# Attention and SwiGLU on one core: seven PSUM banks as one tensor, and a shifted array made on GpSimd

## The chip, the cores and the metric

The kernel runs on one core of one Trainium2 chip. The metric is the device time of one execution in microseconds; three runs of the kernel before are known. A profile of one more execution shows the engines: PE (TensorE), PEld (its weight loads), DVE (VectorE), ACT (ScalarE), POOL (GpSimd) and SP (SyncE, which issues most DMAs).

## The reference

For x of 2048 rows and 512 columns (bf16), 32 heads of 16 columns:

```python
qkv = x @ wqkv                                    # q, k, v for 32 heads
scores = einsum("bhqd,bhkd->bhqk", q, k) * 16 ** -0.5
a = (softmax(scores) @ v, heads put together) @ wo
b = (silu(x @ w_gate) * (x @ w_up)) @ w_down      # 1792 wide
g = sigmoid((x * gate_w).sum(-1))
return g * a + (1 - g) * b
```

The head size of 16 makes the exponentials of 32 x 2048 x 2048 scores the bulk of the work.

## The kernel before, in words

The attention is cut into 32 *units*: four blocks of 512 queries by eight groups of four heads. A unit has 16 *key tiles* of 128 keys, so there are 512 key tiles. The scores of a key tile are four banks of PSUM, one for each head, with the 128 keys on the partitions and 512 queries along the bank.

Each key tile goes one of two ways.

- **ScalarE's way.** `choose()` and `emit_group()` make a *score group*: two matmuls (`score()`) into two neighbouring banks `s_t`, then one exponential of 128 x 1024 into `e_all`, of which 22 banks' worth are kept. Two such double tiles are used in turn (`WIDTHS = (2, 2)`).
- **VectorE's way.** `emit_d()` makes the scores of one head into a single bank `d_t`. Such a matmul can *ride* with a score group: it uses other rows of the array than the two heads of the group. VectorE reads the bank once (`first()` in `emit_d`: a multiplication and an addition, written as 16-bit integers, so that the bits are an approximate exponential in bf16) into a quarter of an array y of 2048 columns. When the four banks of a key tile are in, VectorE refines the approximation. A *four-array* tile (`groups[n] == 4`) gets three copies of y, shifted by integer additions of 25, 56 and 94 (`copy()`), and the four arrays together stand for the exponential. A *two-array* tile (`groups[n] == 2`) gets two bit masks (`bits()`) and one product (`product()`). `quad()` decides: a four-array tile is taken when TensorE has had `SPARE` us to spare. The arrays lie in seven homes (`take_home()`, `home()`, `drop()`); the seventh is part of `wd_t` or `kaug`, so that the profile names these too.

The *PV steps* (`pv()`) multiply with the values, four matmuls in four column tiles into `o_ps`: one step for a key tile of ScalarE, two or four for one of VectorE. When all steps of a unit are done it is closed (`close()`, `post()`), normalised and projected. The FFN's matmuls, the projections for q, k and v, and the output are chains of *pieces* that a `Pacer` gives out by deadlines.

All the order is settled when the kernel is built. A planner in Python keeps a clock for each engine (`plan.pe`, `plan.dve`, `plan.act`), adds a price for each instruction, and emits the one that fits next; `ordered()` ties each instruction to the one before it on its engine, so the engines run just this order, each waiting where its data is late. Prices: 0.217 us for a slot on TensorE, `FLIP` 0.105 us each time that its tiling changes between score groups (rows) and the others (columns), 0.6 us for a bank read or a copy on VectorE, 1.135 us for a product, 0.064 + 0.4265 us per bank for an exponential. `fill_dve()` chooses VectorE's next work: bank reads (`d_wait`, paid by `pay_d()`), copies and the like (`vops`, `pay_v()`), or evictions for the other chains (`owed`, `later()`, `pay()`). `v_unit()` and `wants()` say whether VectorE can take another key tile: it does as long as its own clock lets it finish in time, so the split between ScalarE and VectorE follows from the prices.

PSUM has eight banks. One holds `o_ps`. Four are the two double tiles `s_t`, three (`NM = 3`, `m_tile()`, `m_free()`) are single banks for `d_t` and all chains. Each is a tile of its own pool, and the framework derives the waits from the tiles. GpSimd only fills constants at the start.

In the profile nearly all instructions have the line of a helper (L168 `mm`, L171 `act`, L180 VectorE and the queue), so groups are told apart by tile names.

Of the kernel before, what the change touches and what calls it, by code (L numbers as in the profile page):

```python
# [13 lines left out]
U16 = mybir.dt.uint16  # L14
F16 = mybir.dt.float16
# [64 lines left out]
def kernel(  # L80
# [35 lines left out]
    EB = 10  # L116
    NE = 22
    WIDTHS = (2, 2)
    NM = 3
# [11 lines left out]
    MUL_US = 1.135  # L131
    LATEST = 0.64
# [3 lines left out]
    SPARE = 0.3  # L136
# [12 lines left out]
    ps_s = ctx.enter_context(tc.tile_pool(name="ps_s", bufs=1, space=bass.MemoryType.PSUM))  # L149
    ps_m = [ctx.enter_context(tc.tile_pool(name=f"ps_m{i}", bufs=1, space=bass.MemoryType.PSUM)) for i in range(NM)]  # L150
    ps_o = ctx.enter_context(tc.tile_pool(name="ps_o", bufs=1, space=bass.MemoryType.PSUM))


    last_of = {}

    def ordered(ins):
        i = ins.ins
        if i.engine in last_of:
            tc.add_manual_dep(
                i, last_of[i.engine].name,  # L160
                mybir.DependencyInfo(mybir.DependencyClass.NoSync, mybir.DependencyReason.DATA),
                reason="order",
            )
        last_of[i.engine] = i
        return ins

    def mm(*args, **kw):
        return ordered(nc.tensor.matmul(*args, **kw))  # L168

    def act(*args, **kw):  # L170
        ordered(nc.scalar.activation(*args, **kw))  # L171

    class Ordered:
# [4 lines left out]
        def __getattr__(self, name):  # L178
            f = getattr(self.engine, name)
            return lambda *a, **kw: ordered(f(*a, **kw))  # L180

    vec = Ordered(nc.vector)
    queue = Ordered(nc.sync)
# [99 lines left out]

    kb = const.tile([P, NB], F32, name="kb")
# [8 lines left out]
    class Plan:  # L293
        pe = dve = act = 0.0
# [8 lines left out]
    banks = [0.0] * NM  # L303
    held = [None] * NM
    s_free = [0.0] * len(WIDTHS)
    turns = [0]

    def s_tile(i, name):
        return ps_s.tile([P, WIDTHS[i] * QBW], F32, tag=f"s{i}", name=name)
# [12 lines left out]
    def later(cost, f, ready=None, key=None):  # L322
# [5 lines left out]
        owed.insert(sum(o[0] <= ready for o in owed), (ready, cost, f, c, key))  # L328

    def spend_v(cost, ready=0.0, key=None):  # L330

        if key is not None and key == plan.last:
            cost += 0.13
        plan.last = key
        plan.dve = max(plan.dve, ready) + cost

    def pay(i=0):
        ready, cost, f, c, key = owed.pop(i)
        spend_v(cost, ready, key)
        keep, plan.chain = plan.chain, None  # L340
        f()
        plan.chain = keep
# [18 lines left out]
    def m_tile(name):  # L361
        while m_ready() is None:
            stuck()
        i = min((i for i in range(NM) if banks[i] is not None), key=lambda i: banks[i])
        plan.pe = max(plan.pe, banks[i])
        banks[i] = None
        held[i] = ps_m[i].tile([P, QBW], F32, tag=f"m{i}", name=name)
        return held[i]

    def m_free(ps, t):  # L370
        i = [h is ps for h in held].index(True)
        banks[i], held[i] = t + DVE_PE, None

# [10 lines left out]
    def force(c):  # L384
        for a in c.after + c.begun:
# [146 lines left out]
    def q_pieces(qb, b):  # L532
# [11 lines left out]
        def end(p, me):  # L544
# [7 lines left out]
            def mag():  # L552
# [3 lines left out]
                later(0.21, weigh, plan.dve, ("q", b))  # L556
# [5 lines left out]
            later(0.21, mag, plan.dve, ("q", b))  # L562
# [3 lines left out]
    def q0_pieces(qb):  # L566
# [3 lines left out]
        def landed(p):  # L570
            st["p"] = p
            later(0.6, mag, key=("aq", qb))
            later(0.21, clear, key=("aq", qb))
# [20 lines left out]
    def variants(p, to, q, more=()):  # L594
# [10 lines left out]
        later(0.4, select, key=key)  # L605
# [3 lines left out]
    def gate_end():  # L609
# [8 lines left out]
        later(0.5, end, plan.act + ACT_DVE)  # L618
# [113 lines left out]
    def choose():  # L732

        i = turns[0] % len(WIDTHS)
        if s_free[i] is None:
            flush_act()
        late = max(plan.pe, horizon() - LATEST, s_free[i])
        w = WIDTHS[i]
        if au == UNITS - 1:
            w = min(w, 4 * (hi[au] - at_) - quarter)  # L740
        want = wants()
        open_ = sorted(b for b in banks if b is not None and b <= late)
        n = max(0, min(want, len(open_) - int(side_bank()), 3 - len(d_wait)))
        fit = len(fitting(w)) if n else 0
        n = min(n, fit) if fit or thirst() >= 1.0 else min(n, 1)
        return w, n, max(s_free[i], open_[n - 1]) if n else s_free[i]
# [13 lines left out]
    def emit_group(w, ride, rel):  # L760
        nonlocal quarter, at_, begun
        bs = next_banks(w)
        begun = 1
        i = turns[0] % len(WIDTHS)
        turns[0] += 1
# [4 lines left out]
        s_free[i] = None  # L770
        e0 = e_run(w)
        e_next[0] = e0 + w
        s_t = s_tile(i, "s_t")
        riders = fitting(w)[:ride] if ride else []
        extra = ride and not riders
        if extra:
            riders = d_slots()[:1]
        for k, b in enumerate(bs):
            score(s_t[:, k * QBW:(k + 1) * QBW], b, 32 if riders or w != 2 else 64)
            e_of[b] = e_all[:, e0 + k, :]  # L780
            e_slot[b] = e0 + k
        for k in riders:
            emit_d(k)
# [4 lines left out]
        def exp():  # L788
            act(out=e_all[:, e0:e0 + w, :].rearrange("p w q -> p (w q)"), in_=s_t[:, 0:w * QBW], func=ACT.Exp, scale=inv_sqrt_dh)
            plan.act = max(plan.act + ACT_FIX, ready + ACT_IN) + ACT_COL * w  # L790
            s_free[i] = plan.act + ACT_PE
# [53 lines left out]
    def emit_d(i, rows=32):  # L845
# [6 lines left out]
        left.remove(i)  # L852
        d_t = m_tile("d_t")
        score(d_t[:, :], 4 * n + i, rows)
        if not left:
            vcur.clear()

        def first():
# [5 lines left out]
            m_free(d_t, plan.dve)  # L864
            cur[0] -= 1
# [6 lines left out]
            else:  # L872
                users[h][0] = 2
# [3 lines left out]
        d_wait.append((plan.pe + UNIT_US + PE_DVE, first, n))  # L877
# [9 lines left out]
    def copy(n, k, i, y):  # L887
# [3 lines left out]
        if k == 3:  # L891
            drop(i, plan.dve + 0.05)
            y_live[0] -= 1
# [20 lines left out]
    def pay_d():  # L914
        ready, f, _ = d_wait.pop(0)
        spend_v(0.6, ready)
        f()

    def pay_v():
        cost, f, key, _, _ = vops.pop(0)  # L920
        spend_v(cost, 0.0, key)
        f()

    def fill_dve():

        while plan.dve <= plan.pe + 0.2:
            now = plan.dve
            due = [k for k, o in enumerate(owed) if o[0] <= now + 0.05]
            free = [k for k in due if owed[k][4] is None or owed[k][4] != plan.last]
            fit = bool(vops) and vops[0][3] // KT <= closed + AHEAD and c_ready() <= now  # L930
            if fit and vops[0][3] // KT < au and vops[0][2] != plan.last:
                pay_v()
            elif d_wait and d_wait[0][2] // KT < au and d_wait[0][0] <= now + 0.05:
# [3 lines left out]
            elif d_wait and d_wait[0][0] <= now + 0.05:  # L937
# [118 lines left out]
    def recip(qb, g1, n0):  # L1056
# [21 lines left out]
        at.setdefault(n0 + 6, []).append(lambda: later(1.1 if full else 0.87, spread))  # L1078
        for b in range(g1 // 2):
# [3 lines left out]
            at.setdefault(n0 + 13 + b, []).append(lambda norm=norm: later(0.345, norm))  # L1083
# [28 lines left out]
    def tail_ready():  # L1112
# [5 lines left out]
        al = s_tile(turns[0] % len(WIDTHS), "al")  # L1118
        turns[0] += 1
        a_ps.append(al)  # L1120
# [22 lines left out]
    first = s_tile(0, "first")  # L1143
    kp0 = first[:, 0:2 * QBW]
# [555 lines left out]
```

## Time and profile before

| | us |
|---|---|
| median of three runs | 769.22 |
| lowest, highest | 768.71, 769.77 |
| profiled execution | 768.54 |
| its span, first to last instruction | 766.8 |
| ScalarE busy | 750.8 (98%) |
| TensorE busy | 740.6 (97%) |
| VectorE busy | 734.6 (96%) |
| GpSimd busy | 10.6 (1%) |

The granted TensorE clock is 0.999 over the span. What is outside the span (1.7 us) is not seen by the profile. Durations of neighbouring instructions of one engine overlap by some hundredths of a microsecond, so the price of an instruction on a full engine is the distance from its start to the next start. A matmul's end is modelled.

### The profile page before, as it was taken

How to read it: one execution, taken by the hardware profiler on the slowest of the kernel's cores; microseconds unless marked ns; L12 is line 12 of the kernel's file. 1: busy time of each engine (PE TensorE's matmuls, PEld its weight loads, DVE VectorE, ACT ScalarE, POOL GpSimd, SP SyncE). 2: the span in 40 equal slices, each digit the busy share in tenths (PEclk: the TensorE clock that was granted, in tenths of full speed). 3: DMA queues.
4: the chain of work that ended last, by engine and by line, in shares of the span. 5: the costliest groups of instructions: out<-in, count | busy, mean ns of one | idle time of the engine just before them, and what ended most of it. 6: DMA issues, size and time to landing. Idle time of an engine off the chain costs nothing.

```text
span 766.8 us, 24169 instructions
## 1 busy us (share of the span) xinstructions
PE 740.6 (97%) x10109; PEld 246.0 (32%) x10109; DVE 734.6 (96%) x1234; ACT 750.8 (98%) x843; POOL 10.6 (1%) x25
## 2 busy tenths in 40 slices
PE   8999999999999999999999999999999999999997
PEld 3333333333333233333333333323333333333332
DVE  7899999999999999999999999999999999999993
ACT  6999999999999999999999999999999999999996
POOL 5000000000000000000000000000000000000000
PEclk9999999999999999999999999999999999999999
DMA  9000313144210013211200130212000232100001
GB/s 222 6 2 15 67 21 78 34 117 87 62 28 13 17 41 78 58 33 28 51 18 24 32 95 21 69 28 56 12 19 17 69 80 56 31 18 7 22 30 35
DMA packets 91029, 34.53 MB, mean 45 GB/s; under 512 B 75488, under 2 KB 90472, under 8 KB 90920
## 3 DMA queue, kind: packets, MB, share of 16 engines
q1 hardware_dynamic: 89192, 32.66, 17.7%
q8 instruction: 79, 1.29, 0.7%
q10 hardware_dynamic: 1728, 0.33, 0.2%
q14 instruction: 30, 0.25, 0.1%
HBM read 21.55 MB, written 2.35 MB: 31 GB/s over the span
## 4 chain that ended last, share of the span: by engine, by line
ACT 48%; PE 27%; DVE 13%; issue 11%; DMA 0%; DVEq 0%; ACTq 0%
ACT e_all L171 45%; DVE c_t L180 9%; PE s_t L168 9%; PE o_ps L168 8%; PE gu L168 5%; ACT th L171 2%; PE dps L168 2%; DVE kaug L180 1%; PE qp L168 1%; DVE mt L180 1%; PE vp L168 1%; PE warm L168 1%; DVE gs L180 1%; DVE osb L180 1%; PE kp L168 0%
## 5 line engine op out<-in xcount | busy, mean ns | idle before, releaser
L171 ACT ACTIVATE e_all<-s_t 128x1024 bf16<-128x1024 f32 x774 | 722.9, 1049 | 3.2 <-PE s_t L168 1.6
L180 DVE TENSOR_SCALAR c_t<-d_t 128x512 uint16<-128x512 f32 x432 | 285.8, 681 | 4.8 <-PE d_t L168 4.5
L168 PE MATMUL s_t<-qx,kaug 32*128 32x512 bf16 (+1 forms) x1224 | 237.6, 385 | 11.6 <-ACT e_all L171 10.2
L168 PE MATMUL o_ps<-e_all,vaug 128*32 128x512 bf16 (+3 forms) x2024 | 170.1, 334 | 0.8 <-ACT e_all L171 0.6
L168 PEld LDWEIGHTS <-kaug 32*128 32x128 bf16 (+1 forms) x2048 | 80.6, 91 | 275.8 <-issue 268.6
L180 DVE TENSOR_SCALAR c_t<-c_t 128x2048 uint16<-128x2048 uint16 x236 | 157.7, 682 | 0.4
L168 PE MATMUL d_t<-qx,kaug 32*128 32x512 bf16 x408 | 153.2, 384 | 0.3 <-DVE qx L180 0.3
L168 PEld LDWEIGHTS <-vaug 128*32 128x32 bf16 x4112 | 101.9, 95 | 131.8 <-issue 94.7
L168 PE MATMUL o_ps<-c_t,vaug 128*32 128x512 bf16 (+3 forms) x1768 | 136.3, 341 | 0.7 <-DVE osb L180 0.6
L168 PE MATMUL gu<-xT,wg 128*32 128x512 bf16 x896 | 71.9, 383 | 0.1
L168 PE MATMUL gu<-xT,wu 128*32 128x512 bf16 x896 | 70.2, 383 | 0.0
L168 PE MATMUL ops<-wd_t,mt 128*32 128x512 bf16 x672 | 58.1, 382 | 0.0
L180 DVE TENSOR_SCALAR kaug<-d_t 128x512 uint16<-128x512 f32 x60 | 40.0, 682 | 0.9 <-PE d_t L168 0.7
L180 DVE SCALAR_TENSOR_TENSOR mt<-gs,gu 128x512 bf16<-128x512 bf16 x56 | 38.1, 680 | 1.6
L180 DVE TENSOR_TENSOR c_t<-c_t 128x2048 bf16<-128x2048 bf16 x32 | 38.8, 1214 | 0.0
L168 PE MATMUL s_t<-q,kaug 32*128 32x512 bf16 (+1 forms) x188 | 36.4, 385 | 2.4 <-ACT e_all L171 2.2
L180 DVE SCALAR_TENSOR_TENSOR gs<-th,gu 128x512 bf16<-128x512 bf16 x56 | 38.0, 678 | 0.1
L171 ACT ACTIVATE th<-gu 128x512 bf16<-128x512 f32 x56 | 35.0, 624 | 0.0
L168 PEld LDWEIGHTS <-mt 128*32 128x32 bf16 (+1 forms) x1037 | 25.0, 95 | 26.2 <-issue 19.6
L180 DVE TENSOR_SCALAR kaug<-c_t 128x2048 uint16<-128x2048 uint16 x46 | 31.3, 680 | 0.0
L180 DVE TENSOR_SCALAR c_t<-kaug 128x2048 uint16<-128x2048 uint16 x42 | 28.1, 683 | 0.0
L168 PEld LDWEIGHTS <-wg 128*32 128x32 bf16 x896 | 18.1, 94 | 25.3 <-issue 21.3
(142 smaller groups left out, 434.1 us busy)
## 6 DMA issues: line engine op xcount, KB each, us to landing
wg<-in_B_w_gate_dram SPq DMA_DIRECT2D x56, 128.0 KB
wu<-in_B_w_up_dram SPq DMA_DIRECT2D x56, 128.0 KB
on<-osb SPq DMA_DIRECT2D x120, 16.0 KB
rb<-rr SPq DMA_DIRECT2D x15, 128.0 KB
wd_t<-in_B_w_down_dram SPq DMA_DIRECT2D x7, 256.0 KB
qx<-qst SPq DMA_DIRECT2D x96, 16.0 KB
qx<-aq SPq DMA_DIRECT2D x96, 16.0 KB
out_dram<-o_t SPq DMA_DIRECT2D x12, 128.0 KB
```

What stands on the lines that cost most here:

```text
L168: return ordered(nc.tensor.matmul(*args, **kw))
L171: ordered(nc.scalar.activation(*args, **kw))
L180: return lambda *a, **kw: ordered(f(*a, **kw))
```

## The change

**PSUM.** The two double tiles and the three single banks become one tensor `psum` of seven banks. A score group may take any two or three neighbouring free banks, and one VectorE read may take two. `choose()` weighs every placing by a value with constants for width, riders, hunger of VectorE (`thirst()`) and banks left free.

**Waits.** `ordered()` is told what an instruction reads and writes. For each bank it keeps the last user, makes a wait on it when it is on another engine, finds the other dependences by regions of the SBUF tiles, and tells the framework to derive none of its own for instructions that touch PSUM.

**GpSimd.** Of a four-array tile VectorE makes only the copies shifted by 25 and 56. The copy shifted by 94 is made by `lifted()` on GpSimd, in pieces of one or more banks, as an addition of 32-bit integers (two 16-bit values each) with a broadcast constant. `beside()` puts a piece into GpSimd's queue just before VectorE's next PSUM read, if it fits that read by the planner's prices; it waits for VectorE's last instruction that touches SBUF alone (`fast=True`, `fast_last`). The planner holds such instructions of VectorE until GpSimd's clock `plan.pool` is past. `own_now()` lets VectorE make pieces that are left when it has nothing else.

Further, some constants differ: the reach of PV steps behind the scores (`EB`), the credit of the chains, and `SPARE`. The start uses banks 0 to 6 explicitly.

```diff
-    EB = 10
+    EB = 9
-    WIDTHS = (2, 2)
-    NM = 3
+    NP = 7
+    D_US = (0.0, 0.6, 1.133)
+    HUNGRY = 0.107
+    KEEP = 2
+    FED = 6.808
+    W3 = -0.964
+    N1 = 6
+    N2 = 0.964
+    LOW = 1.12
+    EXTRA = 1.481
+    NEXT = 1.017
+    BURST = 8.876
+    SHORT = 17
+    W3T = 0.087
-    SPARE = 0.3
+    SPARE = 0.253
...
+    psum = ps_b.tile([P, NP, QBW], F32, name="psum")
...
+        for b in uses:
+            j, user[b] = user[b], i
+            if j is not None and j.engine != i.engine and all(j is not k for k in keep):
+                tc.add_manual_dep(i, j.name, SYNC, reason="bank")
+                keep.append(j)
...
+        tc.declare_no_dep(i, group="banks", keep=keep, reason="ordered bank by bank")
...
+    lift = const.tile([P, 2], U16, name="lift")
+    nc.gpsimd.memset(lift[:], int(SHIFTS[2]))
...
+    GPS = 1
+    OWN = 1
+    POOL_IN, POOL_FIX, POOL_ONE, POOL_PE, POOL_OVER = 0.12, 0.09, 0.45, 0.2, 0.1
...
+    def spend_v(cost, ready=0.0, key=None, fast=False):
...
-        plan.dve = max(plan.dve, ready) + cost
+        plan.dve = max(plan.dve, ready, plan.pool if fast else 0.0) + cost
...
     def choose():
-        i = turns[0] % len(WIDTHS)
...
+        hunger = max(0.0, min(1.0, (FED - fed) / FED))
...
+        for w in range(2, most + 1) if most > 1 else (1,):
+            fit = len(fitting(w))
+            for n in range(min(want, 2) + 1):
+                if n > fit and (fed >= LOW or n > 2):
+                    continue
+                p = place(w, n, late)
+                if p is None:
+                    continue
+                free = NP - w - sum(b is None for b in banks) - sum(b is not None and b > late for b in banks)
+                value = (W3 + W3T * min(fed, 4.0)) * (w - 2) + hunger * (0.0, N1, N2)[n] - EXTRA * (n > fit) + NEXT * min(free - n, 3)
+                if best is None or value > best[0]:
+                    best = (value, *p)
...
-            vec.tensor_scalar(out=y[:, i * QBW:(i + 1) * QBW], in0=d_t[:, :], scalar1=EXP_A, scalar2=EXP_B[groups[n]],
-                              op0=ALU.mult, op1=ALU.add)
+            vec.tensor_scalar(out=y.rearrange("p (h q) -> p h q", q=QBW)[:, cols, :], in0=psum[:, i:i + w, :], scalar1=EXP_A,
+                              scalar2=EXP_B[groups[n]], op0=ALU.mult, op1=ALU.add)
...
-                for k in range(1, 4):
+                for k in range(1, 4 - GPS):
                     vops.append((0.6, lambda k=k: copy(n, k, h, y), ("y", n) if k == 1 else None, n, True))
...
+    def lifted(n, m=1, own=False):
...
+        if own:
+            spend_v(0.07 + 0.1335 * m, 0.0, None, True)
+            vec.tensor_scalar(out=c[:, cols], in0=y[:, cols], scalar1=SHIFTS[2], scalar2=None, op0=ALU.add)
+            fast_last[0] = last_of[vec.engine.engine]
+        else:
+            ins = gps.tensor_tensor(out=c[:, cols].bitcast(I32), in0=y[:, cols].bitcast(I32),
+                                    in1=lift[:, :].bitcast(I32).broadcast_to([P, m * QBW // 2]), op=ALU.add)
+            if fast_last[0] is not None:
+                tc.add_manual_dep(ins.ins, fast_last[0].name,
+                                  mybir.DependencyInfo(mybir.DependencyClass.Sync, mybir.DependencyReason.DATA), reason="beside reads of PSUM")
+            plan.pool = max(plan.pool, plan.dve + POOL_IN) + POOL_FIX + POOL_ONE * m
...
+    def beside(span):
+        if not jobs or plan.pool > plan.dve + 0.05:
+            return
+        n = next(iter(jobs))
+        left = sorted(jobs[n][4])
+        if not left or jobs[n][3] is None and min(c_free) > plan.dve:
+            return
+        m = int((span + POOL_OVER - POOL_IN - POOL_FIX) / POOL_ONE)
...
     def fill_dve():
...
+            if plan.pool > now + 0.1 and (slow or d_due):
+                fit = False
+                due = slow
...
+            if not urgent and (d_due or free and not owed[free[0]][5]):
+                beside(span(now))
...
+            elif OWN and plan.pool <= now and own_now(now):
+                pass
...
     def wants():
-        if len(d_wait) >= 3 or not vcur and v_unit() is None:
+        if sum(d[3] for d in d_wait) > 1.3 or not vcur and v_unit() is None:
             return 0
-        return 2 if thirst() < 1.5 else 1
+        return min(2, len(d_slots()))
```

More of the change, by code (lines that the diff above doesn't have):

```diff
@@ L320, in spend, with later @@
         plan.mode = mode
[L322 removed]
+    def later(cost, f, ready=None, key=None, fast=False):
         c = plan.chain
@@ L372, in m_free, with runs, single, left @@
         banks[i], held[i] = t + DVE_PE, None
+    def runs(w, now):
+        ok = [b is not None and b <= now for b in banks]
+        return [(i, s) for s in (1,) for i in range(NP - (w - 1) * s) if all(ok[i + k * s] for k in range(w))]
+    def single():
+        first = min(b for b in banks if b is not None)
+        now = max(first, plan.pe)
+        open_ = [i for i in range(NP) if banks[i] is not None and banks[i] <= now]
+        def left(i):
+            keep, banks[i] = banks[i], None
+            n = len(runs(3, 1e9))
+            banks[i] = keep
+            return n
+        return max(open_, key=lambda i: (left(i), -banks[i]))
     def emit_piece(c):
@@ L1209 @@
     plan.dve = plan.pe + 3.9
+    for i in range(4):
+        banks[i] = 0.0
     pace = Pacer()
```

349 lines of the change are left out of this document (254 added, 95 removed).

## The prediction

> **What bounds the kernel now.** I read the page's first part, then the stretches of 120 us, the groups of instructions, the timeline around 400 us, and the waits.
>
> ```profile
> PE 740.6 (97%) x10109; PEld 246.0 (32%) x10109; DVE 734.6 (96%) x1234; ACT 750.8 (98%) x843; POOL 10.6 (1%) x25
> 120.00:240.00 120.00, 116.18 (x1616) 38.89 (x1612) 116.48 (x193) 119.35 (x137) 0.00 (x0) 1.00 0.28 65
> 240.00:360.00 120.00, 116.86 (x1624) 39.79 (x1621) 119.47 (x197) 119.72 (x136) 0.00 (x0) 1.00 0.17 41
> 360.00:480.00 120.00, 116.74 (x1594) 38.30 (x1586) 119.00 (x192) 119.89 (x136) 0.00 (x0) 1.00 0.16 40
> 480.00:600.00 120.00, 117.68 (x1643) 38.35 (x1640) 117.60 (x191) 119.80 (x135) 0.00 (x0) 1.00 0.15 37
> 600.00:720.00 120.00, 116.70 (x1631) 38.00 (x1627) 119.06 (x198) 119.80 (x136) 0.00 (x0) 1.00 0.16 39
> ```
>
> The columns of a stretch are its length, then PE, PEld, DVE, ACT and POOL busy. ScalarE is busy 598.6 of 600 us, VectorE 591.6, TensorE 584.2, GpSimd not at all. Three engines are full together: the end comes sooner only if ScalarE is given less, VectorE can take that over, and TensorE can follow. TensorE has about 16 us in 600 unused.
>
> ```profile
> L171 ACT ACTIVATE e_all<-s_t 128x1024 bf16<-128x1024 f32 x774 | 722.9, 1049 | 3.2 <-PE s_t L168 1.6 <-ACT e_all L171 0.5 <-PE d_t L168 0.4
> L180 DVE TENSOR_SCALAR c_t<-d_t 128x512 uint16<-128x512 f32 x432 | 285.8, 681 | 4.8 <-PE d_t L168 4.5
> L180 DVE TENSOR_SCALAR kaug<-d_t 128x512 uint16<-128x512 f32 x60 | 40.0, 682 | 0.9 <-PE d_t L168 0.7
> L180 DVE TENSOR_SCALAR wd_t<-d_t 128x512 uint16<-128x512 f32 x8 | 5.5, 685 | 0.3
> L180 DVE TENSOR_SCALAR c_t<-c_t 128x2048 uint16<-128x2048 uint16 x236 | 157.7, 682 | 0.4
> L180 DVE TENSOR_SCALAR kaug<-c_t 128x2048 uint16<-128x2048 uint16 x46 | 31.3, 680 | 0.0
> L180 DVE TENSOR_SCALAR c_t<-kaug 128x2048 uint16<-128x2048 uint16 x42 | 28.1, 683 | 0.0
> L180 DVE TENSOR_SCALAR wd_t<-c_t 128x2048 uint16<-128x2048 uint16 x6 | 4.1, 681 | 0.0
> L180 DVE TENSOR_SCALAR c_t<-wd_t 128x2048 uint16<-128x2048 uint16 x5 | 3.4, 685 | 0.0
> L180 DVE TENSOR_TENSOR c_t<-c_t 128x2048 bf16<-128x2048 bf16 x32 | 38.8, 1214 | 0.0
> L180 DVE TENSOR_TENSOR kaug<-c_t,kaug 128x2048 bf16<-128x2048 bf16 x4 | 4.9, 1213 | 0.0
> L180 DVE TENSOR_TENSOR c_t<-kaug,c_t 128x2048 bf16<-128x2048 bf16 x3 | 3.7, 1217 | 0.0
> L180 DVE TENSOR_TENSOR c_t<-wd_t,c_t 128x2048 bf16<-128x2048 bf16 x1 | 1.2, 1212 | 0.0
> ```
>
> These groups give the split of the 512 key tiles. ScalarE's 774 exponentials of two banks are 387 tiles of four banks; VectorE's first reads are 432 + 60 + 8 = 500 banks, so 125 tiles. The 40 products mark 40 two-array tiles, the other 85 have four arrays. The copies agree: 236 + 46 + 42 + 6 + 5 = 335 = 3 x 85 + 2 x 40.
>
> ```profile
> 399.42 9.34 ACT L171 ACTIVATE e_all<-s_t 128x1024 bf16<-128x1024 f32 x10
> 402.06 1.21 DVE L180 TENSOR_TENSOR c_t<-c_t 128x2048 bf16<-128x2048 bf16 x1
> 403.19 0.68 DVE L180 TENSOR_SCALAR c_t<-d_t 128x512 uint16<-128x512 f32 x1
> 403.79 0.68 DVE L180 TENSOR_SCALAR c_t<-c_t 128x2048 uint16<-128x2048 uint16 x1
> 404.39 1.28 DVE L180 TENSOR_SCALAR c_t<-d_t 128x512 uint16<-128x512 f32 x2
> 405.59 0.68 DVE L180 TENSOR_SCALAR kaug<-c_t 128x2048 uint16<-128x2048 uint16 x1
> 401.22 0.39 PE L168 MATMUL o_ps<-kaug,vaug 128*32 128x512 bf16 x4
> 401.54 0.39 PE L168 MATMUL s_t<-qx,kaug 64*128 64x512 bf16 x2
> 401.86 0.40 PE L168 MATMUL o_ps<-e_all,vaug 128*32 128x512 bf16 x4
> 402.08 0.60 PE L168 MATMUL ops<-wd_t,mt 128*32 128x512 bf16 x8
> ```
>
> From start to start, which is what an instruction costs a full engine: a read of a bank 0.60 us (403.19 to 403.79), a copy 0.60, a product 1.13; an exponential 0.92 (ten in 9.34 us, of which the last one's own 1.05 is taken off: 8.3 over nine). On TensorE a score group between column matmuls costs 0.32 + 0.32 - 0.22 = 0.42 us, because the change of tiling is paid on both sides, and one PV step 0.22. The planner's own constants (0.6, 1.135, 0.917, 0.217 with a flip of 0.105) are these numbers, so what it plans is what runs.
>
> **The change part by part.**
>
> *The last copy goes to GpSimd.* VectorE loses one copy for each four-array tile: 85 x 0.60 = 51 us. GpSimd gets up to 340 one-bank additions of 256 int32 with two inputs. No row shows such an addition; the nearest are these:
>
> ```profile
> L254 POOL MEMSET kaug<- 128x1024 f32 x3 | 2.7, 957 | 0.0
> L264 POOL TENSOR_SCALAR_AFFINE_SELECT ident<-ident 128x128 bf16<-128x128 bf16 x1 | 0.3, 292 | 0.0
> L280 POOL MEMSET sel_t<- 128x4 bf16 x1 | 0.1, 101 | 0.0
> ```
>
> Fixed part 0.10; per element 0.84 ns where nothing is read (957 - 101 over 1024), 1.49 ns where one input is read (292 - 101 over 128). For 256 elements: 0.32 us by the first, 0.48 by the second, and if a second input costs a pass like the first, 0.10 + 256 x 2.33 ns = 0.70. The plan charges 0.54, which lies nearest to the row that reads; I take 0.54 because the plan's other prices are those of the trace. [...]
>
> The waits: a piece waits for VectorE's last SBUF-only instruction (the sync on fast_last), and behind it on GpSimd's queue stand only later pieces; PV of the fourth array waits for it. The plan starts a piece 0.12 us after a read begins and holds the next SBUF-only instruction of VectorE until the piece is over: 0.12 + 0.54 - 0.60 = 0.06 us behind a single read, nothing where another PSUM read follows. VectorE's queue has about 700 PSUM reads of all kinds for roughly 330 SBUF-only instructions, so I let 200 of some 300 pieces be followed by one: 200 x 0.06 = 12 us. Bounds: nothing if pieces cost 0.48, 200 x 0.22 = 44 us at 0.70. VectorE's relief is 51 - 12 = 39 us.
>
> The fourth array is later by a microsecond or two. PV steps of other tiles hide that; without them it would cost up to 0.54 us at each of the 31 closes of a unit, 17 us. I cost it at nothing, as TensorE's list of ready PV steps seldom runs dry (its wait on e_all for o_ps is 0.6 us in all).
>
> *The banks.* Read as code, choose() never takes three banks: W3 + W3T x 4 = -0.62 at best, and the width also loses the term for free banks. Nor two riders: N2 is 0.964 against N1 = 6 at the same hunger. So exponentials stay at two banks, VectorE's first reads at one (the pair of D_US is for the drain), and nothing comes from the wider forms. What remains is that a score group may take any two neighbours of seven banks.
>
> ```profile
> PE s_t L168 <- ACT e_all L171: 13.8, 38, 1.0
> PE o_ps L168 <- ACT e_all L171: 0.6, 1, 0.6
> DVE c_t L180 <- PE d_t L168: 4.5, 11, 0.8
> ```
>
> TensorE waited 13.8 us, 38 times, for the one double tile whose turn it was. That wait can go at most altogether, and as much could be added where readers of shared banks now hold each other; I take 5 us of it as TensorE time won. Writing the waits bank by bank instead of tile by tile changes no other duration: nothing, the same producers and consumers wait on each other.
>
> *What the relief buys.* The plan gives VectorE more tiles. Each tile taken from ScalarE saves it 2 x 0.92 = 1.85 us, so a gain g needs 0.54 g tiles. On VectorE a two-array tile costs 4 x 0.60 + 2 x 0.60 + 1.13 = 4.73, a four-array tile now 3.6. On TensorE a moved tile takes away two groups (0.84) and adds one PV step (two arrays, net -0.63) or three (four arrays, net -0.19); turning a four-array tile into two saves 0.43 there and costs VectorE 1.13. TensorE too must fall by g, less the 5 us: g - 5 = 0.63 x 0.54 g + 0.43 y, so y = 1.53 g - 11.6 tiles turned. VectorE: 4.73 x 0.54 g + 1.13 y + g = 39, that is 5.3 g - 13 = 39, and g = 9.8. Without the 5 us g = 7.4; if TensorE does not limit at all (3.6 x 0.54 g + g = 39), 13; with the full 51 us as well, 17. I take 9.5.
>
> The smaller edits (EB 9, BURST, SHORT, SPARE 0.253, HUNGRY) shift which work fills a gap and add none; SPARE lower makes four-array tiles likelier by 0.05 us of slack each. Nothing for them, with 3 us either way. The start (first exponential at about 12 us) and the tail are as they were.
>
> Sum: the profiled execution took 768.5 us (span 766.8), the median of the three is 769.2. 768.5 - 9.5 = 759.0, as a median about 759.5.
>
> **The rivals.**
>
> *GpSimd holds VectorE back* (slower). The order on every engine is fixed when the kernel is built and VectorE is planned full, so what a piece lasts beyond 0.54 us comes back at each of the 200 SBUF-only instructions behind one, and through the late reads at TensorE and ScalarE. The plan's end of 759.5 then moves by 200 x the excess: 0.70 us gives 200 x 0.16 = 32 us, 791; the point of no gain is 10 / 200 = 0.05, a piece of 0.59 us. For it: two inputs, and no row of GpSimd that reads two. Against: the plan's other prices agree with the rows. [...]
>
> *TensorE is the bound.* It is 97.4% busy in the middle; if the flexible banks win nothing there and the extra PV steps of four-array tiles stay, g is 3 or less: 766. For it the 584 of 600; against, that a moved tile lightens TensorE as well.
>
> *TensorE follows freely.* g of 13 to 17: 752 to 756.
>
> **How the numbers follow.** My forecast (755 to 765) 0.47; TensorE free 0.18; TensorE bound 0.13, a third of it within what can't be told from no change (0.2%, 1.5 us); GpSimd's hold 0.22, of which half is above 778. So faster 0.73, same 0.05, slower 0.22. The range leaves out that upper half and a few hundredths below: 749 to 778. The forecast's own range is 755 to 765.
>
> **What would show it.** ScalarE's exponentials fall to 755 to 765, all still 128x1024 but the last; VectorE's first reads rise to 510 to 530, all but a few 128x512; its 2048-wide copies fall from 335 to about 260; GpSimd shows some 300 TENSOR_TENSOR of about 0.5 us, about 160 us busy. ScalarE stays above 99% in the middle. Wrong, if GpSimd's piece lasts over 0.6 us, if VectorE shows idle time released by GpSimd or SBUF-only instructions well over 0.68 us, or if ScalarE waits for scores in the middle by more than a few us; wrong the other way, if three-bank exponentials or paired reads appear in number.

## The result, and the profile after

The changed kernel took 764.17 us in the median of four runs (763.18 to 765.53), the kernel before 768.99 us in its four on the same chip: a ratio of 0.9936, 95% interval 0.9924 to 0.9948. The same kernel was run once more as the control of the experiments (below): 765.12 us, ratio 0.9943 (0.993 to 0.9955). The change makes the kernel faster by 4 to 5 us. The forecast was 9.5.

Two profiled executions of the changed kernel are used here. The first took 765.53 us (span 763.8), the slowest of its runs; the second took 763.19 us (span 761.5), and is held against the profile of before, which took 768.5 us (span 766.8). First the page's busy times, of the first execution:

```profile
PE 744.7 (98%) x10201; PEld 241.6 (32%) x10201; DVE 718.6 (94%) x1190; ACT 744.6 (97%) x835; POOL 192.3 (25%) x312
```

and the stretches of 120 us of the second (columns as before: length, PE, PEld, DVE, ACT, POOL, granted clock):

```profile
120.00:240.00 120.00, 117.62 (x1640) 37.40 (x1642) 115.63 (x185) 119.28 (x138) 28.50 (x43) 1.00 0.28 65
240.00:360.00 120.00, 117.28 (x1691) 38.56 (x1683) 115.74 (x188) 119.94 (x137) 34.88 (x56) 1.00 0.18 42
360.00:480.00 120.00, 118.65 (x1627) 37.84 (x1623) 115.92 (x188) 119.84 (x135) 27.61 (x45) 1.00 0.18 45
480.00:600.00 120.00, 119.05 (x1659) 38.49 (x1660) 116.21 (x188) 119.86 (x135) 30.01 (x46) 1.00 0.13 32
600.00:720.00 120.00, 117.87 (x1633) 38.12 (x1624) 117.03 (x187) 119.66 (x136) 31.35 (x50) 1.00 0.16 40
```

ScalarE is as full as before (598.6 of 600 us). TensorE rose from 584.2 to 590.5, and VectorE, which was to stay full, fell from 591.6 to 580.5. GpSimd now works in every stretch of the middle, 152 us of the 600. The groups of instructions, each shape by itself, of the first execution (form and count, then busy time, mean ns of one, and idle time before):

```profile
L255 ACT ACTIVATE e_all<-psum 128x1024 bf16<-128x1024 f32 x766 | 716.7, 1044 | 4.0 <-PE psum L252 2.4 <-PE o_ps L252 0.2 <-ACT e_all L255 0.2
L267 DVE TENSOR_SCALAR c_t<-psum 128x512 uint16<-128x512 f32 x440 | 292.6, 683 | 16.3 <-PE psum L252 14.8
L267 DVE TENSOR_SCALAR kaug<-psum 128x512 uint16<-128x512 f32 x72 | 47.9, 683 | 2.1 <-PE psum L252 1.8
L267 DVE TENSOR_SCALAR wd_t<-psum 128x512 uint16<-128x512 f32 x4 | 2.7, 683 | 0.0
L267 DVE TENSOR_SCALAR c_t<-c_t 128x2048 uint16<-128x2048 uint16 x184 | 125.7, 690 | 1.4
L267 DVE TENSOR_SCALAR c_t<-kaug 128x2048 uint16<-128x2048 uint16 x36 | 24.5, 692 | 0.2
L267 DVE TENSOR_SCALAR kaug<-c_t 128x2048 uint16<-128x2048 uint16 x32 | 22.3, 698 | 0.1
L267 DVE TENSOR_SCALAR wd_t<-c_t 128x2048 uint16<-128x2048 uint16 x7 | 4.9, 701 | 0.0
L267 DVE TENSOR_SCALAR c_t<-wd_t 128x2048 uint16<-128x2048 uint16 x2 | 1.4, 683 | 0.0
L267 DVE TENSOR_TENSOR c_t<-c_t 128x2048 bf16<-128x2048 bf16 x34 | 41.5, 1220 | 0.0
L267 DVE TENSOR_TENSOR c_t<-kaug,c_t 128x2048 bf16<-128x2048 bf16 x8 | 9.7, 1216 | 0.0
L267 DVE TENSOR_TENSOR kaug<-c_t,kaug 128x2048 bf16<-128x2048 bf16 x5 | 6.1, 1223 | 0.0
L267 DVE TENSOR_TENSOR c_t<-wd_t,c_t 128x2048 bf16<-128x2048 bf16 x1 | 1.2, 1216 | 0.0
L267 POOL TENSOR_TENSOR c_t<-c_t,lift 128x256 int32<-128x256 int32 x207 | 126.0, 613 | 418.4 <-DVE c_t L267 330.0 <-PE psum L252 31.3 <-DVE kaug L267 24.2
L267 POOL TENSOR_TENSOR c_t<-c_t,lift 128x512 int32<-128x512 int32 x10 | 10.4, 1039 | 8.1 <-DVE c_t L267 7.3 <-DVE kaug L267 0.8
L267 POOL TENSOR_TENSOR c_t<-c_t,lift 128x768 int32<-128x768 int32 x1 | 1.5, 1467 | 0.7 <-PE psum L252 0.7
```

The 766 exponentials are 383 tiles, four fewer than the 387 of before; VectorE's 440 + 72 + 4 = 516 first reads are 129 tiles, four more. The 48 products are 48 two-array tiles, so 81 have four arrays and need 324 one-bank pieces. Over all destinations GpSimd made 286 instructions (269 of one bank, 16 of two, one of three): 304 banks in 182 us. VectorE made the other 20 itself, in nine instructions; three of these are whole copies and stand among the 261 above.

A piece of one bank lasts 0.613 us, and each further bank adds 0.43 (1.039, 1.467), so 0.19 is fixed.

Where the time went, by ScalarE's exponentials, which are nearly unbroken (timeline of ScalarE: start, length, instruction and count); before, first and last row:

```profile
12.52 1.94 ACT L171 ACTIVATE e_all<-s_t 128x1024 bf16<-128x1024 f32 x2 [0.51 <-PE s_t L168]
...
744.68 13.98 ACT L171 ACTIVATE e_all<-s_t 128x1024 bf16<-128x1024 f32 x15
```

and the second execution of after:

```profile
12.98 1.94 ACT L255 ACTIVATE e_all<-psum 128x1024 bf16<-128x1024 f32 x2 [0.49 <-PE psum L252]
...
747.54 4.71 ACT L255 ACTIVATE e_all<-psum 128x1024 bf16<-128x1024 f32 x5
```

The time before the first exponential rose by 0.46 us (12.52 to 12.98); from first to last it fell by 6.8 us (746.1 to 739.3), near the 8 x 0.92 = 7.4 us that eight exponentials fewer are worth; the tail behind the last one, from 758.66 and from 752.25 to the ends of the spans, rose by 1.1 us (8.1 to 9.2). That is 5.3 us between these two executions. The first execution of after has a later start (first exponential at 13.81) and a stretch at half clock, told of below.

### The profile page after: what moved, and what is told of

Same layout as the page of the kernel before. It is cut to its first block, busy times and chain, and to the rows that moved or that the text cites. A ratio compares the mean times of both kernels' runs of the same rounds, so it can differ in the third digit from the quotient of the medians.

```text
span 763.8 us, 24745 instructions
## 1 busy us (share of the span) xinstructions
PE 744.7 (98%) x10201; PEld 241.6 (32%) x10201; DVE 718.6 (94%) x1190; ACT 744.6 (97%) x835; POOL 192.3 (25%) x312
## 4 chain that ended last, share of the span: by engine, by line
PE 51%; ACT 29%; DVE 13%; issue 6%; DMA 1%; DVEq 0%; ACTq 0%
PE psum L252 34%; ACT e_all L255 27%; PE o_ps L252 16%; DVE c_t L267 7%; DVE kaug L267 2%; DVE mt L267 1%; DVE gs L267 1%; ACT th L255 1%; PE warm L252 1%; DVE osb L267 0%; DMA wg<-in_B_w_gate_dram 0%; DVE rd L267 0%; DMA out_dram<-o_t 0%; DVE o_t L267 0%; PE al_o L252 0%
## 5 line engine op out<-in xcount | busy, mean ns | idle before, releaser
L255 ACT ACTIVATE e_all<-psum 128x1024 bf16<-128x1024 f32 x766 | 716.7, 1044 | 4.0 <-PE psum L252 2.4
L267 DVE TENSOR_SCALAR c_t<-psum 128x512 uint16<-128x512 f32 x440 | 292.6, 683 | 16.3 <-PE psum L252 14.8
L252 PE MATMUL psum<-qx,kaug 32*128 32x512 bf16 (+1 forms) x1632 | 253.7, 385 | 8.1 <-ACT e_all L255 5.2
L267 POOL TENSOR_TENSOR c_t<-c_t,lift 128x256 int32<-128x256 int32 (+2 forms) x218 | 137.7, 637 | 427.2 <-DVE c_t L267 337.3
L267 DVE TENSOR_SCALAR c_t<-c_t 128x2048 uint16<-128x2048 uint16 (+2 forms) x188 | 127.0, 683 | 1.6
L252 PE MATMUL psum<-wd_t,mt 128*32 128x512 bf16 x896 | 75.1, 382 | 0.0
L252 PE MATMUL psum<-xT,wg 128*32 128x512 bf16 x896 | 72.2, 384 | 0.1
L252 PE MATMUL psum<-xT,wu 128*32 128x512 bf16 x896 | 71.5, 383 | 0.4 <-DVE c_t L267 0.2
L252 PE MATMUL psum<-q,kaug 32*128 32x512 bf16 (+1 forms) x256 | 50.0, 385 | 0.5 <-ACT e_all L255 0.2
L267 DVE TENSOR_SCALAR kaug<-psum 128x512 uint16<-128x512 f32 x72 | 47.9, 683 | 2.1 <-PE psum L252 1.8
```

The lines of the kernel that those rows point to most:

```text
L252: return ordered(nc.tensor.matmul(out, lhsT=lhsT, rhs=rhs, **kw), [lhsT, rhs], [out])
L255: ordered(nc.scalar.activation(out=out, in_=in_, **kw), [in_, *kw.values()], [out])
L267: return ordered(f(*a, **kw), [v for v in (*a, *kw.values()) if v is not out], [out])
```

## The experiments

The theory on the result: the gain is ScalarE's exponentials alone, and it is smaller than forecast because the banks win nothing, VectorE waits for TensorE, and a stretch of idle TensorE costs clock. The rivals: GpSimd's pieces hold VectorE back; the banks themselves made the gain; the planner's constants made it.

**The control: the changed kernel unedited.**

> The changed kernel as it is, for a second profile. Its four runs lay between 763.2 and 765.5 and the profiled one was the longest, with the first exponential 1.3 us later than before and a stretch at half the TensorE clock. Theory (these two are chance, not the change): 763 to 764, first exponential at 12.5 us, still 766 exponentials. Rival (the one-tensor start costs 1.3 us): the first exponential is at 13.8 us again.

765.12 us, ratio 0.9943 (0.993 to 0.9955), single runs from 763.19 to 765.51: above the theory's 763 to 764. The exponentials, reads and pieces are the same in number. In the profiled execution, the fastest of the five, the start is late too, by 0.46 us instead of 1.3, which lies between theory and rival, and the clock stayed full between start and tail (1.00 in every stretch up to 745 us). The other four have a mean granted clock of 0.998, as the first execution has.

**The banks without GpSimd.**

```
-    GPS = 1
+    GPS = 0
```

> GpSimd's part alone is undone (GPS = 0): VectorE makes all three copies, banks, waits and constants stay as changed. Theory (the whole gain comes from GpSimd's copies; the banks only shift waits): 768 to 770, as before the change. Rival (the seven free banks and the constants carry part of it): 764 to 767.

771.16 us, ratio 1.0029 (1.0017 to 1.004): slower than before, and above both expectations. Its exponentials, in the groups by shape:

```profile
L255 ACT ACTIVATE e_all<-psum 128x1024 bf16<-128x1024 f32 x774 | 723.7, 1040 | 3.1 <-PE psum L252 2.0 <-ACT e_all L255 0.2
```

As many as before, so the same split; the seven banks, their waits and the new choice of work together cost 2 us, and GpSimd's pieces are worth the 6 us from 771.2 to 765.1. TensorE was busy 589.3 of the 600 us in the middle, against 584.2 before, with the same number of score groups: the new banks and choice cost TensorE time instead of winning it. Between the two profiled executions 0.4 us are lost ahead of the first exponential (12.52 to 12.96) and 0.6 behind the last. To see whether the new constants of the planner do that, EB, SPARE and the chains' credit (BURST, SHORT) were put back to the old values as well, and three constants that only the new kernel has were put out of use:

```
-    EB = 9
+    EB = 10
...
-    HUNGRY = 0.107
-    KEEP = 2
+    HUNGRY = -99.0
+    KEEP = 0
...
-    BURST = 8.876
-    SHORT = 17
+    BURST = 3
+    SHORT = 6
...
-    FIRST = 0.087
+    FIRST = -9.0
...
-    SPARE = 0.253
+    SPARE = 0.3
...
-    GPS = 1
+    GPS = 0
```

> GpSimd's part undone as in the run without it, and the constants that both kernels have put back to the old values (EB 10, SPARE 0.3, BURST 3, SHORT 6) or out of use (HUNGRY, KEEP, FIRST); the seven banks, their waits and the choice by value stay. 125 tiles on VectorE, as before the change. Theory (the 2.1 us that the changed kernel without GpSimd lost lie in the banks and the choice): 770 to 772. Rival (they lie in the constants, chosen for the kernel with GpSimd): 768.5 to 769.5.

771.02 us, ratio 1.0022 (1.0013 to 1.0031), 774 exponentials: these constants don't matter here. The 2 us lie in the shared banks, their waits, or choose() and its neighbours; which of them stays open.

**Pieces twice as long.** Each addition is issued twice, the second writing the same values over the first's.

```
-            ins = gps.tensor_tensor(out=c[:, cols].bitcast(I32), in0=y[:, cols].bitcast(I32),
+            first_ = None
+            for rep in range(2):
+                ins = gps.tensor_tensor(out=c[:, cols].bitcast(I32), in0=y[:, cols].bitcast(I32),
...
+                first_ = first_ or ins
+            ins = first_
```

> Every addition on GpSimd is made twice, the second over the first; the order of all engines is the same. A piece then lasts 1.23 us. Theory (an exclusive hold, cheap now because only 63 of 286 pieces have an SBUF-only VectorE instruction right behind the read they start in): these 63 are held 0.6 us longer each, some 90 more about 0.1, so VectorE loses about 45 us, of which its idle time covers some 15: 785 to 800. Rival 1 (no hold, or VectorE is not what the end waits for): under 768. Rival 2 (my forecast's 200 held instructions): 120 us lost, over 840.

821.69 us, ratio 1.068 (1.0656 to 1.0704): between the theory's 785 to 800 and rival 2's 840, so none of the expectations came. The copies of VectorE and ScalarE's wait for scores, in the groups and in the waits (total us, times, longest):

```profile
L267 DVE TENSOR_SCALAR c_t<-c_t 128x2048 uint16<-128x2048 uint16 x184 | 142.3, 780 | 1.4
```

```profile
ACT e_all L255 <- PE psum L252: 48.5, 64, 3.6
```

In the changed kernel the copy lasts 690 ns and that wait is 2.4 us. Over the records, some 155 instructions of VectorE that touch SBUF alone began with more than 0.135 us of an addition left, and were held about 40 us in all (VectorE's busy time is 753.6 us, in the changed kernel 718.6). The time rose by 57, more than the hold. The order is fixed, so a lateness is passed on: TensorE now waited 20.7 us for pieces, and ScalarE for scores. And TensorE's clock fell to half in four places for 3.41 us and in a fifth, near the end, for 6.83. How much each of these adds was not separated.

**Pieces begun without waiting for the SBUF-only instruction ahead.**

```
-            if fast_last[0] is not None:
+            if False:
```

> GpSimd's pieces no longer wait for VectorE's last SBUF-only instruction; they start as soon as their data is in. Order and everything else are the same. Theory (the hold is real and the wait is what keeps pieces under PSUM reads): pieces start under or ahead of VectorE's SBUF-only instructions, some 100 more of these are held by about 0.3 us, VectorE loses 30 us: 770 to 785. [...]

780.7 us, ratio 1.0142 (1.0126 to 1.0157), within the theory's range. Its copies and its pieces:

```profile
L267 DVE TENSOR_SCALAR c_t<-c_t 128x2048 uint16<-128x2048 uint16 x184 | 132.9, 730 | 1.4
...
L267 POOL TENSOR_TENSOR c_t<-c_t,lift 128x256 int32<-128x256 int32 x207 | 155.6, 759 | 391.0 <-DVE c_t L267 343.9 <-PE o_ps L252 24.5 <-PE psum L252 21.2
```

Now both engines are slower where they meet: the piece grows from 613 to 759 ns, the copy from 690 to 730; 96 instructions were held 23 us (VectorE's busy time is 737.1 us against 718.6). So the hold is real and goes both ways, and the wait on fast_last is what keeps it small in the change: there 49 instructions were held, under 3 us in all. A part of the 15.6 us over the control is not the hold: the clock fell to half for 3.41 us here too, at 211.8 and 310.8 us. One of the 49, on VectorE's and GpSimd's timeline of the changed kernel's first execution:

```profile
405.77 0.68 DVE L267 TENSOR_SCALAR c_t<-psum 128x512 uint16<-128x512 f32 x1
406.37 0.79 DVE L267 TENSOR_SCALAR c_t<-c_t 128x2048 uint16<-128x2048 uint16 x1
...
406.00 0.61 POOL L267 TENSOR_TENSOR c_t<-c_t,lift 128x256 int32<-128x256 int32 x1 [12.20 <-DVE kaug L267]
```

The copy begins 0.24 us before the piece ends and takes 0.79 instead of 0.69. The 37 copies that were held in this execution all end 0.55 us after the piece, whether they began with 0.14 or with 0.27 us of it left (0.548 to 0.552), so the last 0.135 us of a piece cost a copy of 0.685 nothing.

**TensorE kept busy where its clock fell.** In the first execution of after, the stretches before and behind 304.1 us (seventh figure after the length, PE, PEld, DVE, ACT and POOL: the granted clock):

```profile
300.70:304.11 3.41, 1.91 (x22) 0.58 (x22) 3.41 (x7) 3.41 (x4) 1.97 (x3) 1.00 0.04 11
304.11:307.52 3.41, 3.41 (x41) 0.94 (x37) 0.97 (x3) 2.28 (x4) 0.92 (x2) 0.50 0.10 24
```

TensorE is 56% busy for 3.41 us and then runs at half clock for 3.41 us; VectorE starves meanwhile (0.97 of 3.41 busy). The work of the 56% is four score groups in a row with only ScalarE's double tile to wait for, here on TensorE's timeline:

```profile
300.81 0.39 PE L252 MATMUL psum<-qx,kaug 32*128 32x512 bf16 x3
301.65 0.39 PE L252 MATMUL psum<-qx,kaug 32*128 32x512 bf16 x3 [0.45 <-ACT e_all L255]
302.57 0.39 PE L252 MATMUL psum<-qx,kaug 64*128 64x512 bf16 x2 [0.52 <-ACT e_all L255]
303.49 0.39 PE L252 MATMUL psum<-qx,kaug 64*128 64x512 bf16 x2 [0.53 <-ACT e_all L255]
```

The experiment issues the scores of these four groups twice, into the same banks with the same values:

```
-            score(psum[:, s[k], :], b, 32 if riders or w != 2 else 64)
+            for _ in range(2 if 283.9 < start < 287.2 else 1):
+                score(psum[:, s[k], :], b, 32 if riders or w != 2 else 64)
```

> Four score groups in the one stretch where TensorE of the changed kernel is least busy (0.56 of the 3.4 us from 300 us on, all others 0.66 or more; in the kernel before no such stretch is under 0.65) make their scores twice, the second over the first; nothing else changes. In the changed kernel's profile TensorE runs at half clock for 3.4 us right behind this stretch. Theory (the stretch trips the clock, and that is the difference between its runs at 763.2 and those at 765): all runs at 763 to 763.8, no half-clock stretch. Rival (the two levels come from the start): runs at both levels again, median 764 to 765.

763.51 us, ratio 0.9928 (0.9914 to 0.9941), all five runs between 763.42 and 764.17 (two of them above the theory's 763.8), where the unedited kernel's nine spread over 763.2 to 765.5. The same stretches of time:

```profile
300.70:304.11 3.41, 2.52 (x26) 0.57 (x26) 3.41 (x7) 3.41 (x4) 1.97 (x3) 1.00 0.04 11
304.11:307.52 3.41, 3.41 (x60) 1.17 (x57) 2.09 (x5) 3.34 (x5) 0.85 (x2) 1.00 0.09 24
```

Work that nobody needs makes the kernel faster: 1.6 us against the control's median, 0.7 against the first four runs. It is the best version found, though its interval overlaps that of the change. The mean granted clocks of the executions agree with the theory: of the unedited kernel's nine, three took 763.2 to 763.3 us at 0.999 or 1.000 and six 764.6 to 765.5 at 0.998; the five with doubled scores are all at 0.999 or 1.000. The rival has a smaller part: the profiled one of these, at 764.17 us, has a late first exponential (13.73), as the first execution of the change has.

**TensorE lightened, in both kernels.** Half of the contraction of the gate and up projections is left out, 928 matmuls of the page's count or, at 0.21 us for four, 49 us of TensorE's work; those outputs are not the reference's.

```
-        return [columns(DC, "gu", ...)
+        return [columns(DC // 2, "gu", ...)
```

Of the kernel before:

> The kernel before with half of the contraction of the gate and up projections left out: 224 column slots, 49 us, fewer on TensorE; the planner knows it. Theory (VectorE bounds the kernel before, TensorE only through the choice between two and four arrays): up to 40 tiles go from two arrays to four, 45 us of VectorE: 755 to 760. Rival 1 (TensorE bounds it): under 750. Rival 2 (neither; the waits in the order keep the split where it is): 764 to 767.

775.09 us, ratio 1.0076 (1.0062 to 1.009): slower, with less to do. All expectations missed. Two of its stretches show why:

```profile
240.00:360.00 120.00, 111.97 (x1411) 36.29 (x1412) 118.95 (x198) 119.47 (x137) 0.00 (x0) 1.00 0.19 46
...
480.00:600.00 120.00, 113.56 (x1464) 36.25 (x1460) 114.65 (x188) 116.49 (x131) 0.00 (x0) 0.97 0.15 36
```

TensorE has gaps now, and in three places (202.8, 486.1 and 656.8 us) the clock fell to half, for 3.41, 6.83 and 3.41 us; where it stayed full, ScalarE is as full as ever. Of the changed kernel (with OWN = 0 besides):

> The same left out of the changed kernel (with OWN = 0, that is, VectorE never makes left-over pieces). Theory (TensorE, 98.4% busy, is what keeps VectorE from spending its relief): 752 or less, over 135 tiles on VectorE. Rival (not TensorE but the order: holds, banks, one rider to a group): within 3 us of the changed kernel with OWN = 0.

777.25 us, ratio 1.0102 (1.0084 to 1.012), outside both expectations, with half clock at 213.4, 264.6 and 616.2 us, for 3.41, 17.07 and 3.41 us. The planner gave VectorE 127 tiles instead of 125 in the first and 130 instead of 127 (the next experiment) in the second. What moved more was the mix: 29 two-array tiles instead of 40 in the first, 26 instead of 47 in the second. Two or three tiles for 49 us: TensorE's work is not what sets the split between ScalarE and VectorE. What a lighter TensorE would be worth without the loss of clock these runs can't say.

**VectorE's own pieces, and the number of double tiles.**

```
-    OWN = 1
+    OWN = 0
```

> The changed kernel with OWN = 0: VectorE never makes left-over pieces of the fourth array. Control for the lighter one. Theory (the left-over pieces are only some 20 banks): 764 to 768, two tiles fewer on VectorE at most. Rival (GpSimd alone can't keep up without them): over 770.

767.03 us, ratio 0.997 (0.9958 to 0.9982), as the theory said; 770 exponentials, 127 tiles. That VectorE may make a piece when GpSimd is late concerns 20 banks of 324, and is worth two tiles: 1.9 us against the control's median, 3.8 against the control's profiled execution, whose clock stayed full; two tiles are 2 x 1.85 us of ScalarE. And

```
-    EB = 9
+    EB = 10
```

> The changed kernel with one constant back at its old value, EB = 10 for 9. 127 tiles on VectorE for 129, 770 exponentials, no stretch of TensorE under 0.7. Theory (the time follows the number of exponentials): four of them more, 3.7 us, less the clock's 1.5: 766 to 768. Rival (EB has no part in it): 763 to 765.

767.07 us, ratio 0.9975 (0.9966 to 0.9985):

```profile
L255 ACT ACTIVATE e_all<-psum 128x1024 bf16<-128x1024 f32 x770 | 719.2, 1048 | 3.6 <-PE psum L252 2.3 <-ACT e_all L255 0.4
```

as the theory said. The "smaller edits" of the prediction are not nothing: with one of them undone, the plan gives VectorE two tiles less, which still lies within the 3 us either way that it allowed.

**GpSimd priced as measured.** The planner's price of a piece becomes 0.187 + 0.426 us for each bank, begun after 0.16, with the last 0.135 us free. A dozen other constants were chosen anew for these prices (EB 8 and NY 4 among them), and where nothing else fits a score group may be made; these edits are not printed.

```
-    POOL_IN, POOL_FIX, POOL_ONE, POOL_PE, POOL_OVER = 0.12, 0.09, 0.45, 0.2, 0.1
+    POOL_IN, POOL_FIX, POOL_ONE, POOL_PE, POOL_OVER = 0.16, 0.187, 0.426, 0.2, 0.2
-        plan.dve = max(plan.dve, ready, plan.pool if fast else 0.0) + cost
+        plan.dve = max(plan.dve, ready, plan.pool - 0.135 if fast else 0.0) + cost
```

> GpSimd's pieces priced as the trace shows them: start 0.16 us after VectorE's read, 0.61 for one bank, 0.43 for each further one, and VectorE's next SBUF-only instruction held only from 0.135 us before the piece's end; a dozen constants chosen anew for this (EB 8, NY 4, LOW 1.59, EXTRA 1.94 and others) so that no 3.4 us of TensorE fall under 0.65. 130 tiles on VectorE, 764 exponentials. Theory (what the end waits for is the number of exponentials, 0.92 us each, and the clock must not trip): 761 to 762.5, no half-clock stretch. Rival (the plan's ends are matched only by luck of an order): 764 to 767.

764.12 us, ratio 0.9937 (0.9924 to 0.9949): no better than the change. The clock stayed full up to the tail (1.00 in every stretch up to 745 us), as expected, but the time missed the 761 to 762.5:

```profile
L255 ACT ACTIVATE e_all<-psum 128x1024 bf16<-128x1024 f32 x764 | 715.5, 1045 | 5.5 <-PE psum L252 3.7 <-ACT e_all L255 0.4 <-PE o_ps L252 0.2
```

Two exponentials fewer (1.8 us), but ScalarE idles more between 120 and 720 us (3.7 us against 1.4 to 2.6 in the two executions of the change), and the first exponential is at 13.68 us. With the right price, and constants chosen for it, the gain is no larger; what the price alone does, among so many edits, isn't shown.

## Why the prediction was right, and where it was off

The direction and the path were right: ScalarE stays the engine that sets the end, the copies moved to GpSimd come back as tiles moved from ScalarE to VectorE, and the time falls. 764.2 lies in the range and just inside the upper end of the forecast's own 755 to 765; the control's 765.1 lies just outside that. The gain is about half of the 9.5 us, and that it isn't further off is in part luck: the hold was put far too high, the banks and VectorE's use of its relief too favourably, and these errors offset each other. By its steps:

**The last copy goes to GpSimd.** Shown: 2048-wide copies fell from 335 to 261 (forecast some 260), first reads rose to 516 (510 to 530), the exponentials to 766 (755 to 765, missed by one), GpSimd makes 286 instructions (some 300) in 182 us (about 160). Taking GpSimd away costs 6 us.

**The piece** lasts 0.613 us, not the 0.54 that was taken because the plan charges it: the plan's prices for instructions that had run before were no evidence for one that had not. It lies inside the bounds of 0.32 to 0.70. The fixed part is 0.19 us and not 0.10, and an element takes 1.67 ns, less than the 2.33 of the upper bound. By the prediction's own test ("over 0.6 us") that should have undone the gain, and it did not, because of the next term.

**The hold** was put at 200 x 0.06 = 12 us, from the plan alone, as no row of before shows one, and measured under 3 us on 49 instructions. Its count was the weak part. Counted over the records, of 286 pieces only 63 have an SBUF-only instruction directly behind the read they begin at; the others have one or more further reads between. And the last 0.135 us are free, so 0.16 us from read to piece, plus 0.613, less the 0.60 of the read, less 0.135 leaves about 0.04 us. By such amounts 63 come to 2.5 us, near what was measured. By the prediction's price and count a piece of 0.613 should have cost 12 + 200 x 0.073 = 27 us.

**The banks** were to win 5 us of TensorE's time. Banks, waits and choice together lose 2 us of the kernel's (the run without GpSimd). The wait that the 5 us came from did go down:

```profile
PE psum L252 <- ACT e_all L255: 6.5, 21, 0.5
DVE c_t L267 <- PE psum L252: 14.8, 30, 2.4
ACT e_all L255 <- PE psum L252: 2.4, 6, 0.6
```

(waits of the changed kernel's first execution: total us, times, longest). 13.8 us became 6.5, but VectorE's wait for TensorE's first reads rose from 4.5 to 14.8. A wait's length was taken as time won, without asking what TensorE would do in it.

**TensorE falls by two groups for each tile moved.** This did not come. Score groups fell from 774 to 766, yet counted by their starts in the records (matmuls of scores over 0.13 us apart, or with other matmuls between, as separate) TensorE makes 800 separate stops for scores instead of 783: 34 of them without an exponential's group, where there were 9. First reads that rode along now get a stop of their own. That 6 us of TensorE's middle went to this was not measured by itself; the run without GpSimd has 807 stops and 5 us more busy time, which fits.

**VectorE stays full** (5.3 g - 13 = 39). The mix of tiles was nearly met: g = 9.5 means 5.1 tiles more and 2.9 turned, so 48 with two arrays and 82 with four; the change has 48 and 81. What failed is that VectorE's time did not fill. By the start-to-start costs its work on tiles was 500 x 0.60 + 335 x 0.60 + 40 x 1.13 = 546 us, and is 516 x 0.60 + 261 x 0.60 + 48 x 1.13 = 520, and 1.5 for those of its own pieces that are not among the 261: 24 less. Of these 5.3 came off the span of the second execution, 11 are idle time in the middle (8.4 to 19.5 us), under 3 the hold, and about 5 are not placed. With the measured hold and nothing won by the banks the same equation would give 5.3 g = 48, g = 9 (an estimate); it has no term for the time in which VectorE waits for TensorE.

**Start and tail as they were.** They were not: 0.5 and 1.1 us later in the second execution.

**The rivals.** GpSimd's hold is there (about 40 us with pieces twice as long, 23 us without the wait, under 3 us in the change), with its break-even in the wrong place. A bound of TensorE gave 766 us, nearer than the forecast, and TensorE is 98.4% busy in the middle. But that TensorE's work limits is not shown: with 49 us less of it the kernel is slower, and the split hardly moves. TensorE following freely is out. No case held the half clock of TensorE after a thin stretch, which costs the change about 1.6 us in six of its nine runs, to go by their mean clocks. Why the plan, with VectorE idle 20 us, doesn't move a fifth tile stays open.

## What to carry over

When work moves to a free engine, count where its neighbours in the order really stand: the mean excess of an instruction times the number that follow it directly, not times all that could. A wait that goes away is a gain only if the engine has something to put in its place, and only if the next engine isn't left waiting; test the part that "should win a little" alone, since here it lost 2 us of the 6 that the other part brought. And look at TensorE and its granted clock in short stretches, not in the average: here 3.41 us that were 56% busy were followed by 3.41 us at half clock, and with that stretch filled by doubled scores the time was 1.6 us under the control's median.

## What was not expected of the hardware

The granted clock fell to half for 3.41 us behind a stretch that was 56% busy, without any of the engine's idle times in it being longer than 0.53 us. The falls of the lightened kernels and of the doubled pieces lasted 3.41, 6.83 and 17.07 us: once, twice and five times as long. The times from change to change are multiples of 3.413 us as well: in the first execution of after 296.96 us (87 times) from the clock's first change at 7.13 us to the fall at 304.09; between the falls of the lightened kernel of before 283.3 and 170.7 us (83 and 50 times), of the lightened changed kernel 51.2 and 351.6 (15 and 103), of the run without the wait 99.0 (29). The first change itself comes at another time in each execution: at 7.13 us in the first of after, at 5.42 us in the second, at 4.45 us in the kernel before. The second execution of the changed kernel has the same thin stretch as the first, a microsecond earlier, and kept its clock:

```profile
299.60:303.01 3.41, 1.91 (x19) 0.39 (x12) 3.41 (x8) 3.41 (x5) 1.96 (x3) 1.00 0.06 14
```

Counted from its 5.42 us, the 87th multiple falls at 302.4 us, inside this stretch, and the 3.42 us ahead of it, from 299.0 us on, are 65% busy (2.23 us). That this place decides was not tried by itself. Where the limit lies is open: the kernel before, with no 3.41 us between 20 and 735 us thinner than 65% (2.22 us busy from 667.6 us on), kept its clock up to 765.6 us. But in the changed kernel lightened and in that with doubled pieces it also fell right behind stretches that the records show 73% to 87% busy (2.48 and 2.56 of the 3.41 us ahead of 213.4 and 616.2 us; 2.59 and 2.98 ahead of 318.3 and 512.8 us), and in the first execution of after 3.42 us that were 45% busy, from 758.06 us on, were followed by 3.41 us at full clock.

On GpSimd, an int32 addition of two inputs, one of them broadcast, took 0.19 us and 1.67 ns for each element (613, 1039 and 1467 ns for 256, 512 and 768), and in the run without the wait, where it met VectorE's SBUF-only instructions more often, the one-bank additions were themselves slowed from 613 to 759 ns in the mean.
